# Late output products of an MLP as seven block products instead of eight, in a kernel whose order of steps is written out

## The chip, the core and the metric

The kernel runs on one core of a Trainium2 chip. The metric is the device time of one execution in microseconds (us). Before the change it is 836.07 us, the median of three runs (836.15, 836.07, 830.36).

## The reference

A gated complex linear recurrence, followed by a two-layer MLP. The two weight matrices come as float64 words, which the kernel turns into float32; all else is float32. Cut to what matters:

```python
# q, k, v, a_re, a_im: (4, 8, 768, 48)
mag = np.sqrt(a_re * a_re + a_im * a_im)
scale = np.minimum(mag, 0.999) / (mag + 1e-06)
a_re_n, a_im_n = (a_re * scale, a_im * scale)
for t in range(S):
    new_re = ar * S_re - ai * S_im
    new_im = ar * S_im + ai * S_re
    S_re, S_im = (new_re + kv, new_im)
    y[:, :, t] = np.einsum('bhd,bhde->bhe', q[:, :, t], S_re)
# x: y as (3072, 384); w_in (384, 2048), w_out (2048, 384)
h = x @ w_in
g = np.maximum(h, 0.0) + alpha * np.minimum(h, 0.0)
return (g @ w_out).astype(np.float32)
```

## The kernel before, in words

The 4 x 768 tokens are 24 chunks of 128, called units. Nine tasks `gates` (letters A to I in the order) make the decays of one to three chunks each from `a_re` and `a_im`, on DVE, ACT and POOL, and write them to DRAM. Tasks J to O load keys, queries, values and weights, and turn the weights into float32 (`loads`, `half_rows`, `loads_v`, `pieces`, `weights`). One task `unit` per chunk (letters P to m) does the recurrence of the chunk in six levels: DVE multiplies keys and queries by decays in place (`step`, L717, the "KQ steps"), ACT copies parts of them (L740, L756), PE multiplies keys by queries (`ps_lv`, L678), DVE and ACT mask the results (L702, L699), PE transposes the keys (`ps_kt`, L785; ACT copies, L787 and L788), forms the chunk's addition to the state (`ps_kv`, L797; DVE L826 and L829) and sums the outputs y of the chunk (`ps_y`, L817 and L841). ACT copies y out (L855) and two DMAs write it to DRAM (L860).

The MLP works on groups of chunks: two single chunks, ten pairs, two single chunks (`sizes`, L642). `loads_x` (L873) loads a group's y as `xT` once its units are done. `features(m, f)` (L881) multiplies `xT` by one of 16 blocks of 128 columns of `w_in`: three matmuls of 256 columns for a pair, of 128 for a single chunk (L889), into one of two PSUM banks `ps_h`; ACT writes relu(-h) (L896) and DVE adds alpha's part (L898), into the ring `g_sb`. `outputs(m, c, f, ...)` (L903) multiplies one block of features of one chunk by a block of `w_out`, 384 columns, and adds up over the 16 blocks in the one PSUM bank `ps_o` (L908); after the last, ACT copies the sum to `top` (L918) and a DMA sends it (L921). `all_mlp` (L926) alternates: one `features`, then up to two `outputs` of earlier features.

PSUM has eight banks of 128 x 512 float32: `ps_h` 2, `ps_lv` 2, `ps_y` 2, `misc` (transposes and state) 1, `ps_o` 1.

What sets the order: every task is a Python generator that issues one instruction (or a few) and yields. `ORDER` is a string of 4,292 letters; `Plan.run` takes the tasks in the order of its letters. No scheduler moves anything afterwards: each engine executes its own instructions in the order in which they were issued, and the waits between engines follow from the tiles that the instructions read and write. The arguments of `yield PE(...)` and the `Ring` objects feed a planner that made the string; in the kernel they do nothing. DMAs are issued from the queue of SP.

## Time and profile before

| | us |
|---|---|
| median of three runs | 836.07 |
| lowest, highest | 830.36, 836.15 |
| the profiled execution | 831.98 |
| its span, first to last instruction | 830.2 |
| PE busy, DVE busy, ACT busy, POOL busy | 692.1, 650.5, 441.5, 215.3 |
| L908 (outputs) on PE, L889 (features) on PE | 294.4, 296.3 |

The granted TensorE clock is 0.991 of full speed over the span. The profile's rows give busy time, the mean duration of one instruction and the idle time ahead of it with the engine that ended it. A float32 matmul is two records on PE and two weight loads (PEld), which overlap PE. The records of pipelined instructions overlap, so sums of means exceed busy time.

### The profile page before, as it was taken

To read this page: it belongs to the slowest core of one execution; us is meant where nothing else is said; L and a number is where in the kernel's file an instruction comes from. 1 tells how busy PE (TensorE), PEld (TensorE's weight loads), DVE (VectorE), ACT (ScalarE), POOL (GpSimd) and SP (SyncE) were. 2 spreads that over 40 slices of the span, in tenths; PEclk is the share of its full clock that TensorE was granted. 3 is DMA by queue.
4 is the path that set the end of the run, shared out by engine and by line. 5 is a ranking of instruction groups with operands and counts; after the bars stand their busy time and mean duration, and the time that the engine had idled before them with its cause. 6 is when DMAs were issued, how large, how long until landed. Compare 5 with 4: busy or idle time off the path is not lost.

```text
span 830.2 us, 26838 instructions
## 1 busy us (share of the span) xinstructions
PE 692.1 (83%) x11488; PEld 525.0 (63%) x11488; DVE 650.5 (78%) x1020; ACT 441.5 (53%) x937; POOL 215.3 (26%) x293
## 2 busy tenths in 40 slices
PE   0001515789999999989999999999999999999998
PEld 0001414567777776767777777777777777777776
DVE  5999999999998899889998988999658644552112
ACT  7758879467636655564576456653443333333121
POOL 5231222617715601460155007310520000000000
PEclk9999997899999999999999999999999999999999
DMA  7597985785688489728874695458535544311110
GB/s 204 177 263 185 279 206 172 228 216 145 157 241 201 114 217 251 181 69 223 245 176 103 171 263 135 120 140 245 148 82 134 150 112 112 92 38 38 35 30 10
DMA packets 194174, 130.91 MB, mean 158 GB/s; under 512 B 74120, under 2 KB 185864, under 8 KB 194056
## 3 DMA queue, kind: packets, MB, share of 16 engines
q1 hardware_dynamic: 194056, 129.20, 58.4%
q8 instruction: 90, 1.47, 0.8%
q14 instruction: 28, 0.23, 0.1%
HBM read 100.82 MB, written 35.71 MB: 164 GB/s over the span
## 4 chain that ended last, share of the span: by engine, by line
PE 68%; DVE 14%; ACT 4%; POOL 4%; DMA 4%; issue 3%; SPq 2%; DVEq 0%; ACTq 0%; POOLq 0%
PE ps_o L908 27%; PE ps_h L889 26%; PE ps_lv L678 4%; PE ps_y L817 4%; DVE KQ L717 3%; PE ps_kv L797 3%; PE ps_y L841 2%; PE ps_kt L785 2%; DVE gate L338 2%; DMA T<-decs 1%; POOL gate L338 1%; POOL gate L340 1%; DVE gate L340 1%; DVE gate L298 1%; DVE gate L426 1%
## 5 line engine op out<-in xcount | busy, mean ns | idle before, releaser
L908 PE MATMUL ps_o<-w_out_sb,g_sb 128*128 128x384 f32 x768 | 294.4, 497 | 9.9 <-DVE g_sb L898 9.0
L889 PE MATMUL ps_h<-xT,w_in_sb 128*128 128x256 f32 (+1 forms) x1344 | 296.3, 353 | 1.2 <-issue 1.2
L889 PEld LDWEIGHTS ps_h<-xT,w_in_sb 128*128 128x128 f32 x1344 | 232.8, 191 | 71.3 <-issue 2.0
L896 ACT ACTIVATE g_sb<-ps_h 128x256 f32<-128x256 f32 (+1 forms) x224 | 79.0, 353 | 221.4 <-PE ps_h L889 220.5
L898 DVE SCALAR_TENSOR_TENSOR g_sb<-g_sb,al,ps_h 128x256 f32<-128x256 f32 (+1 forms) x224 | 97.5, 436 | 120.7 <-ACT g_sb L896 120.1
L908 PEld LDWEIGHTS ps_o<-w_out_sb,g_sb 128*128 128x128 f32 x768 | 136.1, 190 | 61.2 <-DVE g_sb L898 11.6
L717 DVE TENSOR_TENSOR KQ<-KQ,T 96x1024 f32<-96x1024 f32 x120 | 146.8, 1226 | 27.5 <-PE ps_lv L678 24.2
L678 PE MATMUL ps_lv<-WQ 96*32 96x32 f32 x2304 | 34.4, 204 | 77.5 <-DVE WQ L661 54.2
L678 PEld LDWEIGHTS ps_lv<-WQ 96*32 96x32 f32 x2304 | 26.4, 116 | 97.1 <-DVE WQ L661 54.2
L515 POOL TENSOR_SCALAR top<-top 128x768 f32<-128x768 f32 x16 | 44.8, 2802 | 82.3 <-ACT top L507 70.6
L740 ACT COPY WQ<-KQ 96x1024 f32<-96x1024 f32 x48 | 50.0, 1041 | 10.9 <-DVE KQ L717 10.8
L338 POOL TENSOR_TENSOR gate<-gate 128x72 f32<-128x72 f32 x42 | 25.9, 616 | 114.6 <-ACT gate L368 101.9
L338 DVE TENSOR_TENSOR gate<-gate 128x576 f32<-128x576 f32 (+5 forms) x84 | 48.0, 572 | 1.8 <-ACT gate L368 0.3
L756 ACT COPY W<-KQ 96x512 f32<-96x512 f32 x48 | 30.8, 641 | 31.2 <-DVE KQ L717 23.5
L699 ACT ACTIVATE A<-ps_lv,columns 128x64 f32<-128x64 f32 x144 | 38.1, 335 | 16.0 <-PE ps_lv L678 15.8
L817 PE MATMUL ps_y<-A,VL 64*48 64x64 f32 x2304 | 42.7, 224 | 3.9 <-issue 3.9
L855 ACT COPY T<-ps_y 48x256 f32<-48x256 f32 x96 | 31.4, 366 | 24.8 <-PE ps_y L841 23.9
L817 PEld LDWEIGHTS ps_y<-A,VL 64*48 64x48 f32 x2304 | 40.2, 126 | 5.6 <-issue 5.3
L426 DVE TENSOR_TENSOR gate<-gate 128x1152 f32<-128x1152 f32 (+2 forms) x36 | 43.1, 1219 | 0.4 <-POOL gate L411 0.3
L678 PE MATMUL ps_lv<-KQ,W 96*32 96x32 f32 x1536 | 24.9, 204 | 18.4 <-ACT W L756 18.2
L702 DVE TENSOR_TENSOR A<-ps_lv,mask 128x256 f32<-128x256 f32 x96 | 37.8, 413 | 0.0
L785 PE MATMUL ps_kt<-ident,KQ 96*128 96x96 f32 x192 | 25.7, 258 | 14.3 <-DVE KQ L717 9.3
(106 smaller groups left out, 916.1 us busy)
## 6 DMA issues: line engine op xcount, KB each, us to landing
T<-decs SPq DMA_DIRECT2D x48, 384.0 KB
PP<-phs SPq DMA_DIRECT2D x24, 387.0 KB
KQ<-in_q_dram SPq DMA_DIRECT2D x48, 192.0 KB
decs<-gate SPq DMA_DIRECT2D x7, 1152.0 KB
phs<-gate SPq DMA_DIRECT2D x14, 576.0 KB
KQ<-in_k_dram SPq DMA_DIRECT2D x40, 192.0 KB
vsc<-in_v_dram SPq DMA_DIRECT2D x48, 144.0 KB
VL<-vsc SPq DMA_DIRECT2D x24, 288.0 KB
```

What stands on the lines that cost most here:

```text
L338: on(4 * k).tensor_tensor(out=m, in0=w[:, 1::-1].unsqueeze(2).to_broadcast([P, 2, 2, k]), in1=pairs_of(u), op=ALU.mult)
L426: TT(out=m[:, a], in0=U5[:, 1 + a], in1=turned(off3, o)[:, a].unsqueeze(1).unsqueeze(3).to_broadcast([P, L // 2, nb, 2]), op=ALU.mult)
L515: nc.gpsimd.tensor_scalar(out=top, in0=top, scalar1=F64_SMALL, scalar2=None, op0=ALU.max)
L678: nc.tensor.matmul(t[64 * i + j:64 * i + j + HC // 2, p], lhsT=keys(n, g), rhs=queries(n, g), start=True, stop=True)
L717: nc.vector.tensor_tensor(out=x, in0=x if x0 is None else x0, in1=m, op=ALU.mult)
L740: nc.scalar.copy(z.rearrange("p i n t -> p i (n t)").rearrange("p i (m h) -> p m i h", h=h), bass.AP(tensor=KQ.tensor, offset=KQ.offset + ...
L785: nc.tensor.transpose(t[:, p], KQ[:, 1, 4 * i + p], ident[:D2, :D2])
L817: nc.tensor.matmul(o, lhsT=Vp[h][64 * i:64 * i + 64, s, e_ * D:(e_ + 1) * D], rhs=a, start=False, stop=False)
L889: nc.tensor.matmul(p, lhsT=w_in_sb[:, f // 2, kk, f % 2 * P:(f % 2 + 1) * P], rhs=x_of[m][:, kk], start=(kk == 0), stop=(kk == NK - 1))
L896: nc.scalar.activation(gt, p, AF.Relu, scale=-1.0)
L898: nc.vector.scalar_tensor_tensor(out=gt, in0=gt, scalar=al_1[:, f:f + 1], in1=p, op0=ALU.mult, op1=ALU.add)
L908: nc.tensor.matmul(sums[0], lhsT=gt[:, c * P:(c + 1) * P], rhs=w_out_sb[:, f], start=(f == 0), stop=(f == NF - 1))
```

## The change

Pairs 9, 10 and 11 (the last three pairs, `FIRST` to `LAST` - 1; the two single chunks after them are groups 12 and 13) no longer use `outputs`. For a pair, the features are taken as a 2 x 2 matrix of blocks A (two chunks by two halves of the 2,048 features) and `w_out` as a 2 x 2 matrix B (two halves of its rows by two halves of its 384 columns). The four blocks of A B are made of seven block products: with S1 = A21 + A22, S2 = S1 - A11, S3 = A11 - A21, S4 = A12 - S2 and T1 = B12 - B11, T2 = B22 - T1, T3 = B22 - B12, T4 = B21 - T2 the products are A11 B11, S2 T2, S3 T3, S1 T1, A22 T4, A12 B21 and S4 B22.

- `more` (letter p in the order, a new task) makes T1 to T4 on DVE once, in eight subtractions of 128 x 768, in the two buffers that the last `gates` tasks leave.
- `sides` and `fourth` make S1 to S4 of each pair on DVE: eight operations of 128 x 512.
- `group` is one block product: eight matmuls of 192 columns, summed in one half of the bank `ps_o`; the halves alternate from one block product to the next. The bank is taken once for all three pairs.
- `plus` reads a block result on DVE and adds it to a sum in `top`: seven reads a pair, two of them of one result. The first block result is copied by ACT.
- `send` writes a finished chunk to DRAM.
- `product` is the pair's whole sequence; `pump` in `all_mlp` issues half a block product after each `features` of the next pair (or of the single chunk). While half of a pair's features are not there yet, `features` are issued alone.
- `home` puts the features of pairs 9 and 11 into `g_sb`, those of pair 10 and of the last two chunks into a buffer of `gates`.

`ORDER` is replaced by another string, in which all steps are placed anew. The features of all groups, the earlier outputs, the units, the loads and the gates are the same instructions as before. The diff, without the string:

```diff
--- before.py
+++ after.py
@@ -28,49 +28,51 @@
 ORDER = (
...
@@ -202,7 +204,7 @@
     R = {name: Ring(n) for name, n in dict(
         KQ=3, PP=1, T=2, V=1, WQ=2, W=1, run=1, St=3, xT=2, raw0=1, raw1=1, raw2=1, g0=0, g1=0, g2=0, ot=2, top=2,
-        lv=2, misc=1, y=1, h=2, o=1).items()}
+        lv=2, misc=1, y=1, h=2, o=1, z=2).items()}
     for name in LEVELS:
         R[name] = Ring(2 if name <= 4 else 1)
@@ -238,6 +240,7 @@
             return tiny_engine if k <= SMALL else nc.vector
         flat = work.tile([P, 6 * NK * GT], F32, tag="gate", name="gate", bufs=2)[:, 0:6 * N]
+        done["begun", g] = None
         G = flat.rearrange("p (r n) -> p r n", r=6)
         x, c, f, d, e, y = [G[:, i] for i in range(6)]
         dec = flat[:, 3 * N:5 * N].rearrange("p (m s) -> p m s", s=TL)
@@ -873,10 +876,53 @@
             nc.sync.dma_start(x_of[m], ysc_of.pop(m).rearrange("(k p) s -> p k s", p=P))
             done["x", m] = t
+    FIRST = NU // MC - 3
+    LAST = len(sizes) - 2
+    NH = NF // 2
+    DH = DM // 2
+    SIDE = [w_out_sb[:, r * NH:(r + 1) * NH, c * DH:(c + 1) * DH] for r in range(2) for c in range(2)]
+    B11, B12, B21, B22 = SIDE
+    held = {}
+    def more():
+        t = yield DVE(4 * DH, ("begun", len(GATES) - 1), ("gates", len(GATES) - 2), ("w_out", NF - 1))
+        z = work.tile([P, 6 * NK * GT], F32, tag="gate", name="gate", bufs=2)
+        n = NH * DH
+        T1, T2, T4 = [z[:, i * n:(i + 1) * n].rearrange("p (f e) -> p f e", f=NH) for i in range(3)]
+        held["S"] = [z[:, 3 * n + i * NH * P:3 * n + (i + 1) * NH * P].rearrange("p (f s) -> p f s", f=NH) for i in range(2)]
+        held["T"] = [B11, T2, None, T4, B21, T1, B22]
+        one = True
+        for dst, a, b in ((T1, B12, B11), (T2, B22, T1), (T4, B21, T2)):
+            for f in range(0, NH, 4):
+                if not one:
+                    t = yield DVE(4 * DH, t)
+                one = False
+                nc.vector.tensor_tensor(out=dst[:, f:f + 4], in0=a[:, f:f + 4], in1=b[:, f:f + 4], op=ALU.subtract)
+        done["sides", 0] = t
+        for f in range(0, NH, 4):
+            t = yield DVE(4 * DH, t, ("gates", len(GATES) - 1))
+            if f == 0:
+                held["G"] = work.tile([P, 6 * NK * GT], F32, tag="gate", name="gate", bufs=2)
+                T3 = held["G"][:, NF * MT:NF * MT + n].rearrange("p (f e) -> p f e", f=NH)
+                held["T"][2] = T3
+            nc.vector.tensor_tensor(out=T3[:, f:f + 4], in0=B22[:, f:f + 4], in1=B12[:, f:f + 4], op=ALU.subtract)
+        done["sides", 1] = t
     def place(m, f):
         i = (NF * sum(sizes[:m]) + sizes[m] * f) % 36
         return i, R[f"g{i // 12}"], i % 2 if sizes[m] == 1 else None
+    def home(m):
+        k = min(m, LAST) - FIRST
+        if k % 2:
+            return held["G"][:, 0:NF * MT].rearrange("p (f c s) -> p f c s", f=NF, c=MC)
+        i, _, _ = place(FIRST, 0)
+        at = g_sb.rearrange("p r n -> p (r n)")
+        return at[:, i * P:i * P + NF * MT].rearrange("p (f c s) -> p f c s", f=NF, c=MC)
     def features(m, f):
@@ -890,9 +936,14 @@
                              start=(kk == 0), stop=(kk == NK - 1))
         if f == NF - 1:
             R["xT"].put(e)
-        i, ring, half = place(m, f)
-        r = yield ACT(n, e, takes=() if half == 1 else (ring,), first=True)
-        gt = g_sb.rearrange("p r (f s) -> p (r f) s", f=12)[:, i:i + sizes[m]].rearrange("p f s -> p (f s)")
+        if m <= FIRST:
+            i, ring, half = place(m, f)
+            r = yield ACT(n, e, takes=() if half == 1 else (ring,), first=True)
+            gt = g_sb.rearrange("p r (f s) -> p (r f) s", f=12)[:, i:i + sizes[m]].rearrange("p f s -> p (f s)")
+        else:
+            r = yield ACT(n, e, ("sides", 1) if m == FIRST + 1 else ("group", min(m, LAST) - 2, 6), first=True)
+            c = m - LAST if m >= LAST else 0
+            gt = home(m)[:, f, c:c + sizes[m]].rearrange("p c s -> p (c s)")
         nc.scalar.activation(gt, p, AF.Relu, scale=-1.0)
         r = yield DVE(n + 45, r, first=True)
         nc.vector.scalar_tensor_tensor(out=gt, in0=gt, scalar=al_1[:, f:f + 1], in1=p,
@@ -900,6 +951,13 @@
         R["h"].put(r)
         return gt, r
+    def tops_of(m, c):
+        row = (sum(sizes[:m]) + c) * P
+        return tops[0].rearrange("p (c e) -> p c e", c=2)[:, (row // P) % 2], out[row:row + P]
+    scale = 4.0 if words else 1.0
     def outputs(m, c, f, gt, r):
         e = yield PE(0.645, r, ("w_out", f), takes=() if f else (R["o"],))
@@ -907,37 +965,161 @@
             sums[0] = ps.tile([P, DM], F32, tag="o", name="ps_o")
         nc.tensor.matmul(sums[0], lhsT=gt[:, c * P:(c + 1) * P], rhs=w_out_sb[:, f],
                          start=(f == 0), stop=(f == NF - 1))
-        if c == sizes[m] - 1:
+        if c == sizes[m] - 1 and m < FIRST:
             _, ring, half = place(m, f)
             if half != 0:
                 ring.put(e)
         if f == NF - 1:
-            row = (sum(sizes[:m]) + c) * P
+            ot, dst = tops_of(m, c)
             t = yield ACT(DM, e, takes=(R["ot"],))
-            ot = tops[0].rearrange("p (c e) -> p c e", c=2)[:, (row // P) % 2]
-            nc.scalar.activation(ot, sums[0], AF.Copy, scale=4.0 if words else 1.0)
+            nc.scalar.activation(ot, sums[0], AF.Copy, scale=scale)
             R["o"].put(t)
             t = yield DMA(197, t)
-            nc.sync.dma_start(out[row:row + P], ot)
+            nc.sync.dma_start(dst, ot)
             R["ot"].put(t)
+            if c == sizes[m] - 1:
+                done["summed", m] = e
     sums = {}
+    u1, u2, u3 = [tops[1][:, i * DH:(i + 1) * DH] for i in range(3)]
+    def parts(m):
+        A = home(m)
+        A11, A12, A21, A22 = [A[:, r * NH:(r + 1) * NH, c] for c in range(2) for r in range(2)]
+        S1, S2 = held["S"]
+        held[m] = A11, S2, A21, A22, A12, S1, S2
+    def sides(m, r):
+        A11, S2, A21, A22, A12, S1, _ = held[m]
+        for dst, a, b, op in ((S1, A21, A22, ALU.add), (A21, A11, A21, ALU.subtract), (S2, S1, A11, ALU.subtract)):
+            for f in range(0, NH, 4):
+                r = yield DVE(4 * P, r)
+                nc.vector.tensor_tensor(out=dst[:, f:f + 4], in0=a[:, f:f + 4], in1=b[:, f:f + 4], op=op)
+        return r
+    def fourth(m, e):
+        _, S2, _, _, A12, _, _ = held[m]
+        for f in range(0, NH, 4):
+            e = yield DVE(4 * P, e)
+            nc.vector.tensor_tensor(out=S2[:, f:f + 4], in0=A12[:, f:f + 4], in1=S2[:, f:f + 4], op=ALU.subtract)
+        return e
+    def group(m, j, r):
+        for k in range(NH):
+            e = yield PE(0.329, *(() if k else (r, ("sides", 1) if 0 < j < 4 else ("sides", 0))), takes=() if k else (R["z"],) + (R["o"],) * (m == FIRST and j == 0))
+            if k == 0:
+                if m == FIRST and j == 0:
+                    sums["z"] = ps.tile([P, DM], F32, tag="o", name="ps_o")
+                if m not in held:
+                    parts(m)
+                sums["at"] = DH - sums.get("at", DH)
+                z = sums["z"][:, sums["at"]:sums["at"] + DH]
+            nc.tensor.matmul(z, lhsT=held[m][j][:, k], rhs=held["T"][j][:, k], start=k == 0, stop=k == NH - 1)
+            if k == 3:
+                yield "pause"
+        done["group", m, j] = e
+        return z, e
+    def plus(dst, z, u, *e, takes=()):
+        t = yield DVE(DH, *e, takes=takes)
+        nc.vector.scalar_tensor_tensor(out=dst, in0=z, scalar=scale, in1=u, op0=ALU.mult, op1=ALU.add)
+        return t
+    def send(dst, ot, t):
+        t = yield DMA(197, *t)
+        nc.sync.dma_start(dst, ot)
+        R["ot"].put(t)
+    def product(m, made):
+        (ot0, d0), (ot1, d1) = tops_of(m, 0), tops_of(m, 1)
+        yield "need", m, NH - 1
+        z, e = yield from group(m, 0, made[m, NH - 1][1])
+        t1 = yield ACT(DH, e)
+        nc.scalar.activation(u1, z, AF.Copy, scale=scale)
+        R["z"].put(t1)
+        yield "need", m, NF - 1
+        r = yield from sides(m, made[m, NF - 1][1])
+        yield "pause"
+        z, e = yield from group(m, 1, [t1, r])
+        t2 = yield from plus(u2, z, u1, e, t1)
+        R["z"].put(t2)
+        r4 = yield from fourth(m, e)
+        yield "pause"
+        z, e = yield from group(m, 2, [r, t2])
+        t3 = yield from plus(u3, z, u2, e, t2)
+        R["z"].put(t3)
+        yield "pause"
+        z5, e5 = yield from group(m, 5, [r, t3])
+        yield from plus(ot1[:, DH:DM], z5, u3, e5, t3, takes=(R["ot"],))
+        t5 = yield from plus(u2, z5, u2, e5)
+        R["z"].put(t5)
+        yield "pause"
+        z, e = yield from group(m, 3, [r, t5])
+        t = yield from plus(ot1[:, 0:DH], z, u3, e, t3)
+        R["z"].put(t)
+        yield from send(d1, ot1, (t,))
+        yield "pause"
+        z, e = yield from group(m, 4, [made[m, NF - 1][1], t1])
+        t = yield from plus(ot0[:, 0:DH], z, u1, e, t1, takes=(R["ot"],))
+        R["z"].put(t)
+        yield "pause"
+        z, e = yield from group(m, 6, [r4, t])
+        t = yield from plus(ot0[:, DH:DM], z, u2, e, t5)
+        R["z"].put(t)
+        if m == LAST - 1:
+            R["o"].put(t)
+        yield from send(d0, ot0, (t,))
+        yield "pause"
     def all_mlp():
-        made, jobs = {}, [(m, c, f) for m, n in enumerate(sizes) for c in range(n) for f in range(NF)]
+        made, jobs = {}, [(m, c, f) for m, n in enumerate(sizes) for c in range(n) for f in range(NF) if not FIRST <= m < LAST]
+        queue = [[m, product(m, made), None, None] for m in range(FIRST, LAST)]
+        def pump():
+            while queue:
+                m, job, value, wait = queue[0]
+                if wait and wait not in made:
+                    return
+                queue[0][3] = None
+                try:
+                    d = job.send(value)
+                except StopIteration:
+                    queue.pop(0)
+                    continue
+                queue[0][2] = None
+                if d == "pause":
+                    return
+                if isinstance(d, tuple) and d[:1] == ("need",):
+                    queue[0][3] = d[1:]
+                else:
+                    queue[0][2] = yield d
         for m in range(len(sizes)):
+            while queue and queue[0][0] < m - 1:
+                yield from pump()
             for f in range(NF):
                 new = yield from features(m, f)
-                for _ in range(2):
-                    if jobs[0][0::2] not in made:
-                        break
-                    j = jobs.pop(0)
-                    yield from outputs(*j, *made[j[0::2]])
-                    if j[2] == NF - 1:
-                        break
+                if jobs[0][0] < FIRST or not queue:
+                    for _ in range(2):
+                        if not jobs or jobs[0][0::2] not in made:
+                            break
+                        j = jobs.pop(0)
+                        yield from outputs(*j, *made[j[0::2]])
+                        if j[2] == NF - 1:
+                            break
+                if jobs and jobs[0][0] >= FIRST:
+                    yield from pump()
                 made[m, f] = new
+        while queue:
+            yield from pump()
         for j in jobs:
             yield from outputs(*j, *made[j[0::2]])
@@ -960,6 +1142,7 @@
             plan.add(unit(u))
         plan.add(loads_x())
         plan.add(all_mlp())
+        plan.add(more())
         plan.run(ORDER)
 # ---- launch: one core; inputs and outputs as the reference has them ----
```

## The prediction

> **What bounds the kernel now.** I read the page first: the busy shares, the 40 slices and the chain that ended last.
>
> ```profile
> PE 692.1 (83%) x11488; PEld 525.0 (63%) x11488; DVE 650.5 (78%) x1020; ACT 441.5 (53%) x937; POOL 215.3 (26%) x293
> PE   0001515789999999989999999999999999999998
> DVE  5999999999998899889998988999658644552112
> PE 68%; DVE 14%; ACT 4%; POOL 4%; DMA 4%; issue 3%; SPq 2%; DVEq 0%; ACTq 0%; POOLq 0%
> ```
>
> The reader is to see two halves. In the first seven slices (145 us) PE has little to do and DVE is full; later PE is full, and in the last quarter DVE is not. The chain of waits agrees: 68% of it is PE. Next, busy time by stage (us of the stretch, then PE, PEld, DVE, ACT, POOL, each with its instructions):
>
> ```profile
> 300.00:400.00 100.00, 95.17 (x1617) 70.59 (x1616) 90.38 (x123) 57.81 (x119) 24.83 (x44) 1.00 0.69 184
> 600.00:700.00 100.00, 98.37 (x1678) 74.58 (x1672) 62.00 (x87) 36.44 (x101) 4.79 (x8) 1.00 0.46 119
> 700.00:750.00 50.00, 50.00 (x745) 37.10 (x744) 27.07 (x41) 17.93 (x45) 0.00 (x0) 1.00 0.30 76
> 750.00:780.00 30.00, 30.00 (x138) 22.14 (x137) 5.45 (x13) 7.42 (x24) 0.00 (x0) 1.00 0.15 42
> 780.00:800.00 20.00, 20.00 (x249) 15.35 (x248) 3.79 (x10) 3.98 (x13) 0.00 (x0) 1.00 0.12 31
> 800.00:830.20 30.20, 26.66 (x152) 19.97 (x150) 6.24 (x18) 5.98 (x20) 0.00 (x0) 0.99 0.04 14
> ```
>
> From 600 us on, where the three late pairs are worked, PE is idle for 1.6 us before 800 us and for 3.5 us at the very end; DVE is busy 104.6 of 230.2 us, so idle for 125.6. Here a microsecond of matmul is a microsecond of the span, and DVE work is free as long as nobody waits for it. Then the price of a column on PE, from the timeline:
>
> ```profile
> 757.45 1.46 PE L889 MATMUL ps_h<-xT,w_in_sb 128*128 128x256 f32 x6
> 758.74 1.45 PE L908 MATMUL ps_o<-w_out_sb,g_sb 128*128 128x384 f32 x4
> 758.94 0.39 ACT L896 ACTIVATE g_sb<-ps_h 128x256 f32<-128x256 f32 x1 [2.20 <-PE ps_h L889]
> ...
> 795.83 0.83 PE L889 MATMUL ps_h<-xT,w_in_sb 128*128 128x128 f32 x6
> 796.50 1.46 PE L908 MATMUL ps_o<-w_out_sb,g_sb 128*128 128x384 f32 x4
> ```
>
> A matmul is two records. From start to start (the record is longer, its end is modelled) three of 256 columns take 1.29 us, 0.430 each; two of 384 columns from 796.50 to 797.79, where the next row starts, 1.29, 0.645 each; three of 128 columns 0.67, 0.223 each. ACT starts 0.20 us after the next matmul follows the last of a block (758.74 to 758.94).
>
> **The change, part by part.** *PE.* Removed: 3 pairs x 32 outputs x 0.645 = 61.9 us. Added: 3 x 7 block products x 8 matmuls of 192 columns. No row has 192 columns: at the rate of the 256-column rows it is 0.430 x 192/256 = 0.3225 us, at that of the 128-column rows 0.223 x 1.5 = 0.335. I take the middle, 0.329, as 192 lies midway: 168 x 0.329 = 55.3 us. PE gains **-6.6 us**, with ends -7.7 (54.2) and -5.6 (56.3). All of it counts, as PE is full there.
>
> *DVE.* Prices:
>
> ```profile
> L898 DVE SCALAR_TENSOR_TENSOR g_sb<-g_sb,al,ps_h 128x256 f32<-128x256 f32 x160 | 75.6, 474 | 74.1 <-ACT g_sb L896 73.6
> L898 DVE SCALAR_TENSOR_TENSOR g_sb<-g_sb,al,ps_h 128x128 f32<-128x128 f32 x64 | 21.9, 342 | 46.6 <-ACT g_sb L896 46.4
> L426 DVE TENSOR_TENSOR gate<-gate 128x768 f32<-128x768 f32 x4 | 3.7, 952 | 0.0
> L338 DVE TENSOR_TENSOR gate<-gate 128x576 f32<-128x576 f32 x49 | 36.9, 752 | 0.7
> L426 DVE TENSOR_TENSOR gate<-gate 128x384 f32<-128x384 f32 x4 | 2.2, 552 | 0.0
> ```
>
> The weight differences (`more`): 8 of 128x768 at 0.952 = 7.6 us. Sums of features (`sides`, `fourth`): 3 x 8 of 128x512, between 0.552 and 0.752 by columns 0.685, = 16.4 us. The reads of block results (`plus`): 3 x 7 of 128x192 from PSUM, midway between 0.342 and 0.474, 0.408, = 8.6 us. Together 32.6 us in 125.6 idle. ACT loses six evictions of 128x384 (0.491 each, 2.9 us) and gains three of 128x192 (0.276 to 0.384 by L896, about 1.0). I cost this at nothing: its cover is the idle DVE of the table. Were the cover gone, all 32.6 us would be on the path, and the kernel at 860.
>
> *The shared bank.* In the built order the first matmul of a block product waits for the last `plus` on the block before it, though that one lies in the other half of the bank: the halves alternate, but writing and reading do not overlap. Queued behind this wait on PE are the next features and, through them, ACT and DVE. The price: 0.20 us from PE to the reader, 0.408 the read, about 0.05 back (the last L898 of the kernel ends at 825.79, the weight load released by it starts at 825.84) and up to 0.19 for a weight load that can't run ahead (its row: 191 ns): 0.66 to 0.85. Cover: three feature matmuls stand between any two block products, 1.29 us while they are of 256 columns, so the first two pairs wait for nothing if DVE comes at once. The third pair runs among features of 128 columns, cover 0.67: four bare boundaries x 0 to 0.18, I take 0.4 in all. The double read (two `plus` of one result, 1.1 us) has eight or more other matmuls beside it in the third pair. Where a unit's KQ step (L717, 1.226 us) stands ahead of the read, 0.6 more; in the order this is so in one place, the sixth block product of the first pair, behind a KQ step and two mask products (1.226 + 2 x 0.413) that themselves wait for 0.5 us of PE: 3.2 us against 2.84 of cover, 0.4 us.
>
> A rule speaks to this. The Trainium skill (PSUM — Partial Sum Buffer, section PSUM bank collisions raise a hardware error) holds that PE and DVE may not touch one bank at once even at different columns. By it the wait is needed and the sum stands as it is; without it, with reads beside writes, the sum would be 0.8 us lower. No row of before has two engines in one bank, so the trace can't say.
>
> *Thinner filler.* Outputs used to stand two by two between the steps of the late units; now six features of the first late pair and two of the next stand in a row without outputs, and unit 23's transposes meet only features of 128 columns. Features alone: evacuation 0.20 + 0.384 + 0.474 against 1.29, so a KQ step ahead costs up to 0.9; I find two places, 0.2 each. Unit 23: its second transposes and L797 wait for ACT's copies (L787 479, L788 276 ns) with 0.22 to 0.45 of features beside them: about 1.0 us. And one transpose that waits for a KQ step, 0.5. Together 1.9.
>
> Sum of the waits: 0.4 + 0.4 + 1.9 = **+2.7**. Bounds: 0 (all covered; less than nothing through the order, below) and, with one KQ step ahead of each of the 13 boundaries of the first two pairs and the third at its worst, 13 x (0.75 + 1.226 - 1.29) + 0.7 + 1.9 = 11.5.
>
> *The order anew.* Every step may move, so I summed before's rows in the order of each kernel, up to the last KQ step of each unit. DVE: through unit 12 the sums differ by -2.8 to +1.2 us, for units 13 to 18 by -2.2 to +4.9; ACT and POOL by at most 5 us all along; the bytes that SP has issued by at most 2.2 MB of 131 (mostly under 1), 14 us at the mean 158 GB/s. From unit 19 the difference grows to 24 us: the new DVE work. PE work left behind each unit's last matmuls falls by 5.5 to 7.9 us through unit 9 (the gain is 6.6). So up to 600 us the queues are the old ones with small exchanges; I take 0, with -5 to +5 by these differences. On SP the six late output transfers move too; one of them stands ahead of loads of unit 23 (0.4 to 0.6 us of issue each) and waits for a `plus` of the second pair, with some 20 us of PE work between: nothing. The last output waits, as before, for one ACT copy.
>
> **Sum.** The profiled execution took 831.98 us (span 830.2, 1.8 around it). 831.98 - 6.6 + 2.7 + 0 = 828.1. It stands 4.1 below the median 836.07; with the three runs (836.15, 836.07, 830.36) the mean of four is 833.6, 1.7 above it. I add 1.7, as the runs fall on both sides: **829.8**.
>
> **The rivals.** *Slower: reads late behind the units.* At the 13 boundaries of the first two pairs, two KQ steps ahead of the read instead of none: 13 x (0.75 + 2.45 - 1.29) = 24.8, so 831.98 - 6.6 + 24.8 + 1.7 = 851.9. It is slower than before from 0.5 us a boundary on (6.6/13), by over 1% from 1.2. For it: DVE takes 30 us more by unit 23. Against: at 300 to 400 us DVE is 90% busy and PE still 95%. With one step ahead (11.5 in all) it is 838.6.
>
> *Loads bind.* The weight load's records (190 ns, two to a matmul) may not hide under 192 columns: 168 x 0.38 = 63.8, nothing is gained: 838.3. Against: 128-column matmuls with the same loads come every 0.223 us, so loads overlap. The Trainium skill (TensorE: Matmul & The Clock Gate, LDWEIGHTS) has columns/1.2, an estimate of 107 ns here; by that 168 x 0.214 = 36 us, the load never binds, and the trace's 0.223 agrees.
>
> *The order also closes gaps.* PE is idle 10.0 us between 200 and 600 us (windows of 100 us); half of it gone: 824.8. For it: every step is placed anew. Against: the sums by unit hardly differ.
>
> *Not done as told* is excluded: the built order has 168 matmuls of 192 columns and 96 outputs fewer.
>
> **How the numbers follow.** Forecast (waits of 0 to 6, block products at either end: 826 to 834): 0.60. Gaps closed: 0.15. One KQ step ahead: 0.13. Two: 0.08. Loads bind: 0.04. One per cent of 836.07, about what a measurement can tell from no change, is 8.4: faster below 827.7, slower above 844.4. Faster: 0.15 + a quarter of 0.60 = 0.30. Slower: 0.08. Same: 0.62. Range for 8 in 10: 822 to 840.
>
> **What would show it.** Right: 192-column matmuls 0.32 to 0.34 us apart; PE busy near 685; DVE busy some 30 more; PE's waits for `plus` under 2 us in all; the first y matmuls of units 0 to 12 within 5 us of before's. Wrong: waits of PE for `plus` over 7 us; PE idle over 5 us before unit 23; a start that is late by more than 5 us at unit 4.

## The result, and the profile after

The changed kernel takes 828.26 us, the median of 20 runs (825.86 to 834.08), against 835.69 us for 20 runs of before (830.36 to 842.62): a ratio of 0.9923, with a 95% interval of 0.9903 to 0.9943, so 4.8 to 8.1 us less. The prediction was 829.8 (822 to 840). The profiled execution took 827.08 us, its span is 825.1.

The page of the changed kernel, busy shares, 40 slices and chain:

```profile
PE 691.9 (84%) x11632; PEld 547.1 (66%) x11632; DVE 676.1 (82%) x1073; ACT 438.4 (53%) x934; POOL 230.7 (28%) x293
PE   0001435879799999999999999999999999999998
DVE  5999999889899899999999889999769786844321
PE 64%; DVE 17%; POOL 5%; DMA 5%; ACT 4%; issue 2%; SPq 2%; DVEq 0%; ACTq 0%; POOLq 0%
```

PE is still the bound. DVE has 25.6 us more, in the last quarter, as foretold. But the first line holds a trap: PE's busy time is what it was (692.1 before), although 7 us of its work are gone. The runs e2b and e2c below, which have the old products in the new order, show why: there PE is busy for 699.9 and 698.8 us, against 691.9 and 690.3 in two profiles of the changed kernel. So the products do take 7 to 10 us off PE's busy time, and the new order puts about as much on. Part of that is the clock: PE was busy at half clock for 21 us of e2b and for 9 us of before, which makes some 6 us of e2b's busy time (an estimate: half of the difference). Busy time over a whole span compares two kernels of one order, not of two. The stages show more (us of the stretch, then PE, PEld, DVE, ACT, POOL):

```profile
300.00:400.00 100.00, 99.69 (x1779) 74.18 (x1772) 94.60 (x128) 60.46 (x123) 28.64 (x47) 1.00 0.69 185
600.00:700.00 100.00, 99.57 (x1794) 82.67 (x1794) 77.30 (x116) 40.49 (x107) 4.21 (x8) 1.00 0.49 124
700.00:750.00 50.00, 49.77 (x684) 45.31 (x684) 30.46 (x51) 15.40 (x43) 0.00 (x0) 1.00 0.29 69
750.00:780.00 30.00, 28.82 (x329) 27.27 (x328) 11.98 (x28) 6.44 (x21) 0.00 (x0) 1.00 0.05 15
780.00:800.00 20.00, 20.00 (x121) 16.87 (x120) 4.74 (x14) 3.05 (x11) 0.00 (x0) 1.00 0.09 30
800.00:825.10 25.10, 21.60 (x113) 15.44 (x111) 4.17 (x12) 4.30 (x14) 0.00 (x0) 0.98 0.04 16
```

PE stays full beside the new DVE work; before 800 us it idles 1.84 us from 600 us on. What the shared bank costs stands in the view of the line that reads the block results:

```profile
L1029 DVE SCALAR_TENSOR_TENSOR top<-ps_o,top x21: 342/357/358, 668.9 to 787.8; 128x192 f32<-128x192 f32 x21
who waited for it (us, times):
  PEld ps_o L1021: 0.2, 1
```

In all of the 21 reads PE's side waited once, 0.2 us, at 692.5 us. The timeline of the third pair shows how closely that is cut (its rows of PE and DVE):

```profile
778.34 1.47 PE L1021 MATMUL ps_o<-gate,g_sb 128*128 128x192 f32 x8
778.85 0.35 DVE L949 SCALAR_TENSOR_TENSOR gate<-gate,al,ps_h 128x128 f32<-128x128 f32 x1 [1.11 <-ACT gate L947]
779.64 0.83 PE L935 MATMUL ps_h<-xT,w_in_sb 128*128 128x128 f32 x6
779.84 0.36 DVE L1029 SCALAR_TENSOR_TENSOR top<-ps_o,top 128x192 f32<-128x192 f32 x1 [0.64 <-PE ps_o L1021]
780.31 1.51 PE L1021 MATMUL ps_o<-w_out_sb,g_sb 128*128 128x192 f32 x8
```

Four block-product matmuls take 1.30 us from start to start (778.34 to 779.64). The read ends at 780.20 and the next block product starts at 780.31, just when the three narrow feature matmuls (0.67) are through. The four matmuls that begin it take 1.35 us instead of 1.30, as at the other three bare boundaries of this pair: 0.2 in all.

**Where the time went.** For the stretch from the first features of pair 9 to the end I add, on PE, the time from the start of each record to the start of the next; waits fall to the record ahead of them. Beside the changed kernel stands the run e2b below, which has the old products in the same order:

| us | block products | outputs | features | L681 | L820 | other unit steps | sum |
|---|---|---|---|---|---|---|---|
| changed kernel | 56.3 | 36.9 | 86.7 | 10.8 | 8.4 | 14.1 | 213.3 |
| old products, same order (e2b) | 0 | 100.3 | 86.8 | 9.8 | 7.5 | 14.1 | 218.4 |

The outputs of the three pairs fall from 63.4 (100.3 - 36.9) to 56.3 us, by 7.1; 1.9 come back in the products of keys and queries (L681) and the sums of y (L820) of the last units (1.0 in the second profile of the changed kernel, where L681 takes 10.1 and L820 8.2). Before's own stretch is 222.2 us, but it starts with more unit work left, so it does not compare directly.

### The profile page after: what moved, and what is told of

Same layout as the page of the kernel before. It is cut to its first block, busy times and chain, and to the rows that moved or that the text cites. A ratio compares the mean times of both kernels' runs of the same rounds, so it can differ in the third digit from the quotient of the medians.

```text
span 825.1 us, 27168 instructions
## 1 busy us (share of the span) xinstructions
PE 691.9 (84%) x11632; PEld 547.1 (66%) x11632; DVE 676.1 (82%) x1073; ACT 438.4 (53%) x934; POOL 230.7 (28%) x293
## 4 chain that ended last, share of the span: by engine, by line
PE 64%; DVE 17%; POOL 5%; DMA 5%; ACT 4%; issue 2%; SPq 2%; DVEq 0%; ACTq 0%; POOLq 0%
PE ps_h L935 26%; PE ps_o L966 18%; PE ps_o L1021 7%; PE ps_lv L681 4%; DVE KQ L720 4%; PE ps_y L820 3%; PE ps_kv L800 2%; DVE gate L341 2%; PE ps_y L844 2%; PE ps_kt L788 2%; POOL gate L341 1%; POOL top L518 1%; POOL gate L343 1%; DMA PP<-phs 1%; DVE gate L301 1%
## 5 line engine op out<-in xcount | busy, mean ns | idle before, releaser
L966 PE MATMUL ps_o<-w_out_sb,g_sb 128*128 128x384 f32 x512 | 200.6, 504 | 11.8 <-DVE g_sb L949 11.7
L720 DVE TENSOR_TENSOR KQ<-KQ,T 96x1024 f32<-96x1024 f32 x120 | 147.8, 1233 | 19.5 <-PE ps_lv L681 14.4
L947 ACT ACTIVATE g_sb<-ps_h 128x256 f32<-128x256 f32 (+1 forms) x176 | 63.6, 363 | 117.3 <-PE ps_h L935 116.4
L966 PEld LDWEIGHTS ps_o<-w_out_sb,g_sb 128*128 128x128 f32 x512 | 91.1, 192 | 46.1 <-DVE g_sb L949 14.1
L949 DVE SCALAR_TENSOR_TENSOR g_sb<-g_sb,al,ps_h 128x256 f32<-128x256 f32 (+1 forms) x176 | 78.5, 449 | 37.1 <-ACT g_sb L947 36.5
L681 PE MATMUL ps_lv<-WQ 96*32 96x32 f32 x2304 | 34.6, 204 | 70.3 <-DVE WQ L664 54.0
L681 PEld LDWEIGHTS ps_lv<-WQ 96*32 96x32 f32 x2304 | 26.7, 116 | 91.1 <-DVE WQ L664 54.0
L518 POOL TENSOR_SCALAR top<-top 128x768 f32<-128x768 f32 x16 | 50.6, 3171 | 58.9 <-ACT top L510 55.7
L949 DVE SCALAR_TENSOR_TENSOR gate<-gate,al,ps_h 128x128 f32<-128x128 f32 (+1 forms) x48 | 18.7, 391 | 48.9 <-ACT gate L947 48.6
L947 ACT ACTIVATE gate<-ps_h 128x128 f32<-128x128 f32 (+1 forms) x48 | 15.0, 313 | 67.1 <-PE ps_h L935 66.9
L820 PE MATMUL ps_y<-A,VL 64*48 64x64 f32 x2304 | 43.3, 229 | 5.5 <-issue 3.3
L820 PEld LDWEIGHTS ps_y<-A,VL 64*48 64x48 f32 x2304 | 41.0, 129 | 7.0 <-issue 4.6
L681 PE MATMUL ps_lv<-KQ,W 96*32 96x32 f32 x1536 | 24.6, 205 | 21.5 <-ACT W L759 20.8
```

What stands on the lines that cost most here:

```text
L518: nc.gpsimd.tensor_scalar(out=top, in0=top, scalar1=F64_SMALL, scalar2=None, op0=ALU.max)
L681: nc.tensor.matmul(t[64 * i + j:64 * i + j + HC // 2, p], lhsT=keys(n, g), rhs=queries(n, g), start=True, stop=True)
L720: nc.vector.tensor_tensor(out=x, in0=x if x0 is None else x0, in1=m, op=ALU.mult)
L820: nc.tensor.matmul(o, lhsT=Vp[h][64 * i:64 * i + 64, s, e_ * D:(e_ + 1) * D], rhs=a, start=False, stop=False)
L947: nc.scalar.activation(gt, p, AF.Relu, scale=-1.0)
L949: nc.vector.scalar_tensor_tensor(out=gt, in0=gt, scalar=al_1[:, f:f + 1], in1=p, op0=ALU.mult, op1=ALU.add)
```

## The experiments

The stretch from the first features of pair 9 to the end of the span is the cleaner measure: the steps ahead of it are the same in all kernels with the new order, but for four of the eight weight differences, which e2, e2b and e2c lack, and yet it starts anywhere from 610.6 to 616.9 us in them. From each kernel's profile:

| kernel | ratio to before, 95% interval | starts | ends | stretch |
|---|---|---|---|---|
| changed kernel | 0.9923, 0.9903 to 0.9943 | 611.8 | 825.1 | 213.3 |
| r, the same again | 0.9923, 0.9887 to 0.9959 | 610.6 | 823.1 | 212.5 |
| e1, 24 more matmuls | 1.0003, 0.9979 to 1.0027 | 613.3 | 834.4 | 221.1 |
| e2, old products, new order | 1.0034, 1.0003 to 1.0064 | 615.1 | 839.9 | 224.8 |
| e2c, e2 once more, a single run | 836.63 us | 616.2 | 834.5 | 218.3 |
| e2b, old products a step earlier | 1.0008, 0.9977 to 1.0038 | 612.4 | 830.9 | 218.4 |
| e4, no filler between block products | 1.0204, 1.0155 to 1.0252 | 616.9 | 852.9 | 236.0 |
| e8, no filler behind the sums | 1.0055, 1.0026 to 1.0083 | 615.3 | 838.4 | 223.1 |
| e5, 14.8 us more sums | 1.0142, 1.0113 to 1.0172 | 612.8 | 841.5 | 228.7 |
| e6, 14.9 us more DVE, spread out | 0.9914, 0.9884 to 0.9945 | 613.6 | 827.2 | 213.6 |
| e3, new products, old order | 1.0216, 1.0163 to 1.0268 | 609.3 | 849.0 | 239.7 |
| e7, the same, sums earlier | 1.0204, 1.0173 to 1.0235 | 609.2 | 845.6 | 236.4 |

**The changed kernel again (r).** No edit.

> The changed kernel itself, unaltered, once more beside the runs of before that the other kernels of this group share, to see how far its ratio can be trusted. Expected by every theory: 0.992 again, between 0.990 and 0.995.

The same ratio, 0.9923; the stretch of this repeat is 0.8 us shorter.

**Are PE's columns the gain? (e1)**

```diff
+            for _ in range((1 if j else 2) if k == 0 else 0):
+                nc.tensor.matmul(z, lhsT=held[m][j][:, k], rhs=held["T"][j][:, k], start=True, stop=True)
             nc.tensor.matmul(z, lhsT=held[m][j][:, k], rhs=held["T"][j][:, k], start=k == 0, stop=k == NH - 1)
```

> The changed kernel with eight more matmuls of 192 columns in each late pair (the first of each block product is issued twice, that of the first block product three times; the repeats are overwritten), 24 in all, in the same steps of the same order. Nothing else differs. Theory (PE is full where the pairs are worked, and the gain of the change is the columns taken off PE): 24 x 0.322 to 0.329 = 7.7 to 7.9 us more than the changed kernel's 828.3, so about 836, the time of before, ratio 1.000. Rival A (the new order closed gaps and PE has slack there): the repeats fall into idle time of PE, 828 to 830, ratio 0.991 to 0.993. Rival B (the weight load binds at 192 columns, 0.38 a matmul): 9.1 us, 837.4.

837.61 us, and the stretch is 7.8 us longer: 0.325 for each of the 24. PE has no slack, and rival A falls. Against rival B (0.38 a matmul, 9.1 us) neither the time nor a stretch that repeats within 0.8 us is sharp enough; the rows are: four block-product matmuls come every 1.30 us, here as in the timeline above, so the weight load does not bind.

**Is it the order? (e2, e2b, e2c)** In e2 the steps stay and the products go back (an excerpt; the sums and the weight differences are left out):

```diff
-            nc.tensor.matmul(z, lhsT=held[m][j][:, k], rhs=held["T"][j][:, k], start=k == 0, stop=k == NH - 1)
+                for i in range(s * 32 // 56, (s + 1) * 32 // 56):
+                    c, f = divmod(i, NF)
...
+                    nc.tensor.matmul(sums[0], lhsT=home(m)[:, f, c], rhs=w_out_sb[:, f], start=f == 0, stop=f == NF - 1)
```

> The new order with the old output products: in the steps in which the changed kernel issues its 56 block-product matmuls of a late pair, this one issues the 32 output matmuls of 384 columns (chunk by chunk, ACT copies the sums), and neither the sums of features nor the weight differences nor the reads of block results are made; all other steps stand where the changed kernel has them. Theory (gain = columns): 6.6 us more PE work than the changed kernel, less the 0.2 us of waits for reads and at most 1 or 2 us of late evacuations that the missing DVE work gives back: 833 to 835, ratio 0.997 to 0.999. Rival A (the order brought the gain): 828, ratio 0.991.

839.53 us: above both expectations. Its profile has one stop that belongs to neither, with the stretches before, in and after it (PEclk is the third figure from the end):

```profile
686.00:689.30 3.30, 3.30 (x128) 2.54 (x126) 1.50 (x3) 0.44 (x2) 0.00 (x0) 1.00 1.10 255
689.30:692.40 3.10, 0.01 (x1) 0.00 (x0) 1.22 (x1) 0.00 (x0) 0.00 (x0) 0.83 0.55 118
692.40:698.20 5.80, 5.79 (x51) 4.49 (x52) 0.00 (x0) 0.11 (x1) 0.00 (x0) 0.50 0.15 31
698.20:702.00 3.80, 3.80 (x104) 2.79 (x103) 3.23 (x6) 1.52 (x5) 0.00 (x0) 1.00 0.28 69
```

PE stands still for 3.1 us in the middle of 96 equal records (48 matmuls of L820), released by no engine, and then runs 5.8 us at half the clock: about 6 us of the stretch. Two more runs asked whether that is the program's: one as it is, one with the outputs moved by up to a step.

```diff
-                for i in range(s * 32 // 56, (s + 1) * 32 // 56):
+                for i in range(-(-s * 32 // 56), -(-(s + 1) * 32 // 56)):
```

> The same old products in the new order as in the first of these runs, unaltered, for one more profile. If the stop at 689 us belongs to the program: again 2 to 4 us of PE waiting for nothing that the profile shows in the matmuls of the unit at about 689 us, span 837 to 841. If it was chance: no stop there, span 833 to 835.

> Old products in the new order as before, with the 32 output matmuls of a pair rounded up instead of down onto the 56 steps, so that most stand one step earlier; the amounts are the same. Theory (the run before it lost some 5 us to one stop of PE of 3.1 us for no engine at 689 us and the half clock behind it, and that stop hangs on where the instructions fall): without the stop 833 to 835.5, ratio 0.998 to 1.001. Rival H (the old products are slower by 9 us in the new order for a reason in their own waits): 839 again, ratio 1.003 to 1.006.

Neither profile has the stop, and the stretches agree at 218.3 and 218.4. The unaltered program ran without it, so the program does not bring it in every execution; in that the theory put down for e2b was wrong. e2b takes 834.2 us, the time of before. With the old products the new order is worth nothing that 0.3% of resolution shows, in either direction: the gain is not the order's. Between e2b and the changed kernel the ratios differ by 0.85%, some 7 us, and the stretches by 5.1 to 5.9; the intervals of the ratios, 0.2 to 0.4% either way, cover the difference. Where the higher median of e2 over 12 runs comes from stays open; its interval and that of e2b overlap.

**What does the shared bank cost without filler? (e4)**

```diff
         r4 = yield from fourth(m, e)
-        yield "pause"
         z, e = yield from group(m, 2, [r, t2])
...
-                if jobs and jobs[0][0] >= FIRST:
+                if jobs and jobs[0][0] >= FIRST and f % 2:
                     yield from pump()
```

The pause goes at four more places like this one. With half as many, twice as large portions, two boundaries between the pairs lose their filler too: 17 in all.

> The changed kernel with the filler taken away between the block products: the last half of one block product and the first half of the next are issued back to back, after every second block of features, at five of the six boundaries of each late pair, 15 in all (the boundary after the first block product, which also waits for the sums of features, keeps its filler). PE work and its density over the pair stay the same. Theory (the first matmul of a block product waits for the read of the block before it, though that lies in the other half of the bank, and the filler hid this): 15 x 0.66 to 0.85 = 9.9 to 12.8 us, and 1 or 2 us more where the read queues behind other DVE work: 838 to 843, ratio 1.003 to 1.009; the trace shows PE waits for the reads of 0.6 to 1 us each. Rival D (the two halves need no turns, and the filler was not needed): no waits for reads, 828 to 830, ratio 0.991 to 0.993.

854.5 us: the wait is real, and the kernel loses twice what was expected, 22.7 us of the stretch. Its waits on PE from 616 us on:

```profile
PE ps_o L1021 <- DVE top L1029: 12.9, 17, 1.9
PE ps_h L935 <- DVE g_sb L949: 1.0, 1, 1.0
PE ps_y L844 <- DVE St L832: 0.9, 1, 0.9
PE ps_lv L681 <- DVE KQ L720: 0.8, 1, 0.8
PE ps_kv L800 <- ACT T L791: 0.7, 1, 0.7
PE ps_kt L788 <- ACT T L791: 0.7, 1, 0.7
PE ps_h L935 <- DVE gate L949: 0.5, 1, 0.5
```

```profile
712.22 1.46 PE L1021 MATMUL ps_o<-w_out_sb,g_sb 128*128 128x192 f32 x8
712.48 1.22 DVE L720 TENSOR_TENSOR KQ<-KQ,T 96x1024 f32<-96x1024 f32 x1
713.62 0.47 DVE L949 SCALAR_TENSOR_TENSOR gate<-gate,al,ps_h 128x256 f32<-128x256 f32 x1
714.01 0.35 DVE L1029 SCALAR_TENSOR_TENSOR top<-ps_o,top 128x192 f32<-128x192 f32 x1
714.41 1.27 PEld L1021 LDWEIGHTS ps_o<-w_out_sb,gate 128*128 128x128 f32 x8 [1.02 <-DVE top L1029]
714.41 1.57 PE L1021 MATMUL ps_o<-w_out_sb,gate 128*128 128x192 f32 x8 [0.72 <-DVE top L1029]
```

Here a KQ step (L720) holds up the evacuation of the features that were issued before the read (L949, 0.47), the read stands behind both, and the next weight load too waits for it: 2.19 us from start to start instead of 1.30, 0.89 lost. At a bare boundary nothing stands ahead of the read:

```profile
740.78 1.46 PE L1021 MATMUL ps_o<-gate 128*128 128x192 f32 x8
742.28 0.36 DVE L1029 SCALAR_TENSOR_TENSOR top<-ps_o,top 128x192 f32<-128x192 f32 x1 [0.40 <-PE ps_o L1021]
742.69 0.59 PE L1021 MATMUL ps_o<-gate 128*128 128x192 f32 x2 [0.45 <-DVE top L1029]
```

That is 1.91 instead of 1.30, 0.61 lost. From the start of the last matmul of a block product to the next block product, less 0.325, 8 of the 17 boundaries lose 0.61; three with a double read lose 0.87, 0.88 and 1.29; six with a product of 1.22 us of a unit (L720 or L666) ahead of the read lose 0.89 to 2.08. Together that is 15.7 us, 0.93 each. The other 7.0 of the 22.7 lie in units and features, which got two neighbours of a kind (the six smaller waits above, 4.6 us) and one window of half clock; they were not in the expectation. So it is the filler that keeps the price of the shared bank at a few tenths.

**Do the sums need a cover? (e8)**

```diff
         r = yield from sides(m, made[m, NF - 1][1])
-        yield "pause"
         z, e = yield from group(m, 1, [t1, r])
```

> The changed kernel without the filler between the sums of features and the second block product: after the six sums of a pair are issued, the block product that needs them follows at once, with no block of features between; all other fillers stay. Theory (the sums are the step that needs a cover of its own: six operations of 0.615 us, one evacuation of 0.47 ahead of them and at times a KQ step of 1.22): PE stands 3 to 5 us three times and runs slow for some us after a stop of 3 us or more: 9 to 20 us, 837 to 848, ratio 1.003 to 1.015. Rival G (the reads and sums are cheap wherever they stand, DVE has idle time): 828 to 831, ratio 0.991 to 0.995.

837.1 us, at the low end: the stretch is 9.8 us longer. That of pair 11 took most of it, here with the stretches around it (PEclk is again the third figure from the end):

```profile
763.78:767.19 3.41, 0.92 (x10) 0.73 (x8) 2.95 (x6) 1.27 (x4) 0.00 (x0) 1.00 0.00 0
767.19:777.43 10.24, 9.16 (x148) 8.45 (x149) 1.95 (x4) 0.65 (x2) 0.00 (x0) 0.50 0.01 3
777.43:780.84 3.41, 3.41 (x25) 3.41 (x25) 1.98 (x5) 0.55 (x2) 0.00 (x0) 1.00 0.00 0
```

PE stood 3.5 us for the sums, and the clock was then at half for 10.24 us.

**Is DVE's amount hidden, or only its place? (e5, e6)** Both add nearly the same amount of DVE work to the late pairs: e5 in the sums that PE waits for, e6 behind reads, where nobody does.

```diff
-                nc.vector.tensor_tensor(out=dst[:, f:f + 4], in0=a[:, f:f + 4], in1=b[:, f:f + 4], op=op)
+                for _ in range(4 if dst is S1 else 2 if dst is S2 else 1):
+                    nc.vector.tensor_tensor(out=dst[:, f:f + 4], in0=a[:, f:f + 4], in1=b[:, f:f + 4], op=op)
```

> The changed kernel with 24 more DVE operations of 128x512 (eight a pair: the sums S1 are formed four times over and S2 twice, each time with the same values), 24 x 0.615 = 14.8 us more DVE work between the first block product and the second of each pair. Nothing else differs. Theory (the new DVE work lies in idle time of DVE, which has some 90 us idle from 610 us on, and only a read or a sum that PE waits for costs): the sums of a pair end 4.9 us later, against a filler of one block of features and a unit's steps of some 3 to 10 us behind them; 0 to 6 us in all, 828 to 834, most likely 830. Rival E (DVE is on the path there): all 14.8 us, 843.

```diff
+    def again():
+        k = held["k"] = (held.get("k", -2) + 2) % NH
+        _, T2, _, _, _, T1, _ = held["T"]
+        nc.vector.tensor_tensor(out=T2[:, k:k + 2], in0=B22[:, k:k + 2], in1=T1[:, k:k + 2], op=ALU.subtract)
...
         nc.vector.scalar_tensor_tensor(out=dst, in0=z, scalar=scale, in1=u, op0=ALU.mult, op1=ALU.add)
+        again()
         return t
```

(The same call stands behind each of the two late sums.)

> The changed kernel with 27 more DVE operations of 128x384 (nine a pair: after each read of a block result and after each of the two late sums, a piece of a weight difference is formed again with the same values, when nobody waits for it), 27 x 0.552 = 14.9 us, the amount of the run with more sums, but spread out and off the chain. Theory (DVE has room; what costs is only how long the next block product must wait for one read or sum): an extra operation delays a read only where it stands ahead of it (the second of a double read, a feature's second half), by 0.55 us against slacks of 0.1 to 2 us: 0 to 5 us, 828 to 832, ratio 0.992 to 0.998. Rival E (the amount of DVE work is on the path): 15 to 17 us as in the run with more sums, 843, ratio 1.010 to 1.014.

e5 takes 843.66 us, e6 828.59. From 610 to 820 us, first the changed kernel, then e6:

```profile
610.00:820.00 210.00, 208.16 (x2805) 179.16 (x2804) 122.74 (x209) 64.56 (x178) 1.99 (x4) 1.00 0.30 77
610.00:820.00 210.00, 208.04 (x2797) 178.34 (x2795) 136.15 (x237) 65.50 (x181) 1.99 (x4) 1.00 0.30 78
```

and e5:

```profile
610.00:820.00 210.00, 197.71 (x2719) 171.47 (x2718) 136.89 (x225) 62.03 (x169) 1.99 (x4) 0.98 0.30 77
```

DVE has 13.4 us more in e6 and 14.2 in e5, and PE loses 10 us in e5 alone. My estimate for e5 (830) fell: its time is that of rival E, but e6 shows that the amount is not the reason. The 15.4 us by which its stretch is longer are three stops of 4.28, 3.9 and 3.2 us (in the second, a unit's y waits for its state, whose addition stands behind the sums) and three windows of half clock. The first, in its timeline (some rows of PE are left out):

```profile
659.97 5.65 DVE L1000 TENSOR_TENSOR gate<-g_sb 128x512 f32<-128x512 f32 x8
661.61 1.56 PE L935 MATMUL ps_h<-xT,w_in_sb 128*128 128x256 f32 x6
665.53 1.29 DVE L1000 TENSOR_TENSOR g_sb<-g_sb 128x512 f32<-128x512 f32 x2
666.74 2.74 DVE L1000 TENSOR_TENSOR gate<-gate,g_sb 128x512 f32<-128x512 f32 x4
668.20 2.67 PE L1022 MATMUL ps_o<-gate 128*128 128x192 f32 x8 [4.28 <-DVE gate L1000]
```

In the changed kernel the last sum of each pair ends 0.71, 1.10 and 1.54 us before the block product that needs it; 4.9 us more cannot fit.

**Could the old order carry the new products? (e3, e7)** The string of before, with each late output step replaced by the block-product steps that belong to the same features, spread over the same places; e7 adds one block of features behind the sums, in a string spread anew.

```diff
 ORDER = (
-    "AAAAABAAAAAAAAAAAAAAAAAAAMMMMBANNJJMBBAAMABKAKKAAAAKJAAAAAAAAJANNANAALLBALBBAAAAAAAAAAAAAKBAAAOBOAAA"
...
+    "AAABAAAAAMAAAAAAAAAAAAAAAAAMMMBAAAAMJNAAAAAAAANJNNAAABANANAABBAABAJAKJABAAMAAAABBAAAAAABAOAAOAAKABAA"
...
```

> The old order with the new block products: the string of before, in which the steps of the late pairs' outputs are replaced by those of the block products, spread over the same places, features and all units, loads and gates staying where they were; the eight weight differences go in at the same unit step as in the changed kernel. Theory (gain = columns, order neutral): 6.6 us less than before and up to 3 us of waits back, 829 to 832, ratio 0.992 to 0.996. Rival A (the order brought the gain, the products none): 835 to 837, ratio 1.000. Rival C (the new order was needed to hide the reads and sums): over 840, ratio over 1.005.

```diff
         r = yield from sides(m, made[m, NF - 1][1])
         yield "pause"
+        yield "pause"
```

> The new block products in the old order once more, but with one more block of features between the sums of a pair and the first block product that needs them; the steps of the pairs are spread over the old places as before. Theory (in the old order PE stood 5.4 and 2.5 us for the sums of features, and its clock fell behind the longer stop): the 7.9 us and some 2 to 4 us of slow matmuls come back, 842 to 845, ratio 1.007 to 1.010. Rival F (the loss in the old order is spread over units that meet thinner filler): 850 to 856, ratio 1.017 to 1.024.

854.17 and 849.34 us: rival C. In e3 the sums of pair 10 stood behind a KQ step, a mask and the evacuation of their last features:

```profile
724.00 1.21 DVE L720 TENSOR_TENSOR KQ<-WQ,T 96x1024 f32<-96x1024 f32 x1
725.13 0.41 DVE L705 TENSOR_TENSOR A<-ps_lv,mask 128x256 f32<-128x256 f32 x1
725.46 0.47 DVE L949 SCALAR_TENSOR_TENSOR g_sb<-g_sb,al,ps_h 128x256 f32<-128x256 f32 x1
725.85 3.69 DVE L999 TENSOR_TENSOR gate<-gate 128x512 f32<-128x512 f32 x6
729.00 2.93 PE L1021 MATMUL ps_o<-gate 128*128 128x192 f32 x8 [5.40 <-DVE gate L999]
```

In all, PE waited 7.9 us for sums in e3. The extra block of features halved that (3.6), but features then waited 4.9 us for DVE, three times. The stretch of before less the 7.1 us of products would be 215.1; e3 is 24.6 above it, and e7 gave back 3.3. Half clock is a second part: three switches with 10.1 us of PE work in them, some 5 us (an estimate: half of it). So the wait for the sums is one part, and much of the rest is spread over units and features (rival F). These two strings are my own and nobody searched for a good one; they show that the products can't go into the old places as they are, not what the best order of this kind would give.

## Why the prediction was right, point by point

- *PE, -6.6 us: right.* 63.4 us became 56.3, so -7.1; from start to start both kinds are 0.01 to 0.015 us a matmul dearer than the bare prices, as they change places with others. The block-product matmul costs 0.325 us (e1), between 0.3225 and 0.335 as bounded. Loads do not bind.
- *DVE, +32.6 us at nothing: right here, for a reason too weak.* DVE's busy time grew by 25.6. A sum of 128x512 takes 0.605 us in a row, not 0.685, and a read 0.357, not 0.408. Idle DVE does hide the amount (e6: 13.4 us more cost nothing). But what the step called cover, the idle time of DVE, is not what protects the sums: one block of features and a unit's steps do, with 0.7 to 1.5 us to spare, and 14.2 us in the wrong place cost 15.4, half clock included (e5). The sum had no term for the sums' wait; it was nil, by the place the order gives them.
- *The shared bank, +0.8: 0.2 to 0.4.* Both places were named rightly. The one wait for a read (0.2, at 692.5 us) stands at the first pair's sixth block product, behind a KQ step and two masks, where the sum had 0.4; the four bare boundaries of the third pair cost 0.05 each, where it had 0.4 in all. Without filler the chain costs 0.61 (e4), a little under the 0.66 to 0.85 of the sum: the read takes 0.357, and the weight load adds nothing. The Trainium skill (PSUM — Partial Sum Buffer, PSUM bank collisions raise a hardware error) holds that two engines may not touch one bank at once even at different columns. e4's rows show PE waiting while DVE reads the other half. They can't say whether the chip or only the program asks for it; a version without the wait was not tried.
- *Thinner filler, +1.9: the size held by luck, the places not.* e2b and the changed kernel have the same 0.5 us wait of unit 23's L800, so that is no cost of the products. 1.9 us lie in L681 and L820 instead. The waits listed there make up 1.3 (0.4 behind an evacuation, 0.9 for no engine); the rest is not settled. In the repeat the same two lines have 1.0 us more than in e2b.
- *Order anew, 0: right.* e2b has it with the old products and takes before's time. That does not make it idle: it is what keeps the products' waits at nothing (e3, e7). PE's idle time from 200 to 600 us did fall, from 10.0 to 8.0 us, but in e2b it is 7.0, and that kernel is no faster than before.
- *+1.7 from the profiled execution to the runs: too small for before* (835.69 - 831.98 = 3.7 over 20 runs) and about right after (1.2).
- *Indicators.* Waits for reads under 2 us, DVE some 30 more (25.6), matmuls 0.325 apart: held. PE busy near 685: failed (691.9); the forecast started from before's 692.1, but the new order alone has some 699 (e2b, e2c), and the products come off that. The first L844 of units 3 to 8 starts 3.7 to 6.8 us later than before's L841, just over the 5 that was to count as wrong, and the 300 to 400 us stretch makes it up (PE 99.69, before 95.17): it was an exchange, not a loss, and it is the order's (2.6 to 7.3 us in e2b).
- *The slower rival* (reads that come late) is real: with the filler gone the kernel takes 854.5, 15.7 us of it at the boundaries. Six of 17 reads there stand behind a KQ step or a unit's other product of that size, none behind two. It did not come because the order leaves a block of features at each boundary.

## What to carry to other kernels

Work added to an engine with idle time is free in amount, not in place: price it by the slack between its end and the instruction that needs it, step by step, and ask what stands ahead of it in its queue. Trade work on a full engine for work on an idle one only together with an order that puts independent work of the full engine between each hand-over. And price an edit on PE by start-to-start times in the stage where it happens, or against a kernel of the same order; busy time over the span, set against a kernel of another order, hid it here.

## What the runs showed of the hardware

A stop of PE costs more than itself. After most of the stops over 2 us the granted clock was exactly 0.50, for 3.41, 6.83 or 10.24 us, whole multiples of one length. In e5, around the stop of 664 to 668 us:

```profile
661.69:665.10 3.41, 2.24 (x70) 1.67 (x70) 3.27 (x6) 0.38 (x1) 0.00 (x0) 1.00 0.36 86
665.10:668.51 3.41, 0.31 (x2) 0.31 (x3) 3.38 (x6) 0.00 (x0) 0.00 (x0) 1.00 0.31 77
668.51:671.92 3.41, 3.41 (x11) 3.16 (x10) 3.38 (x7) 0.83 (x1) 0.00 (x0) 0.50 0.51 135
671.92:675.33 3.41, 3.41 (x81) 3.01 (x80) 3.34 (x7) 1.42 (x4) 0.11 (x1) 1.00 0.02 4
```

A window in which PE did 0.31 us of work is followed by one at half the clock, which costs 1.7 us at most. The same came after stops of 2.23, 2.54 and 5.40 us (e3), 2.38 (e7), 3.10 (e2) and 3.5 (e8). In each of these the 3.41 us ahead of the switch hold 0.3 to 1.41 us of PE work. After a stop of 1.92 us (e4), and after one of 3.01 us at 211 us in the changed kernel, whose window still held 1.52 us of work, the clock stayed full; twice it fell after more, 1.94 us among transposes (e4) and 1.91 at 259 us (e8). The Trainium skill (TensorE: Matmul & The Clock Gate, Part 1: The HAM clock gate) tells of a free-running window of 3,413 ns and a clock that is either full or half; length and values agree with these rows. It lets the clock fall after an idle window; here windows in which PE was busy up to two fifths of the time, and in two cases over half of it, were idle enough, so the measured rows decide. None of the prediction's prices had a term for it. It makes 4.6 of the 9.8 us in e8 (half of the 9.16 that PE was busy at half clock), at most 5.1 of the 15.4 in e5, and next to nothing in the changed kernel after 176 us.
